# One decode step on one core: the last row of wo with the weight stationary and the output on 128 partitions

## The chip, the cores and the metric

The kernel runs on one core of a Trainium2 chip. Its time is the device time of one execution in microseconds (us); the time before is a median of 3 runs.

## The reference

One token passes through an attention block and an MLP that work in parallel on the same normalised input, and their outputs are added to it:

```python
x = A_x                                   # 1 x 1 x 1024
xn = _layernorm(x)
return x + _A_ref(xn, k_cache, v_cache, wq, wo) + _B_ref(xn, w1, b1, w2, b2)
# A: q = xn @ wq, 32 heads of 128; scores against the last 4096 positions of 4 kv heads,
#    softmax, o = p @ v (4096 numbers), then o @ wo
# B: y = layernorm(xn); h = gelu(y @ w1 + b1) with the tanh form, 3584 numbers; h @ w2 + b2
```

Everything is bf16. The weights, keys and values are about 40 MB and each is read once, for a single token.

## The kernel before

**Loads.** The large transfers go through the queue of SP in a fixed order: k_sb (4 pieces), wq (2), w1 (2), v_sb (3), w2 (2), wo (6). They land in tiles of one pool with four slots, so each later transfer waits until an earlier tile is used up: the last six pieces (L228) need the slots of w1 and v_sb. The 32 rows of wo that a partition holds come as one piece of 16 rows and then as pieces of 8, 4, 2, 1 and 1 rows. The small inputs go through the queue of ACT: x as 128 partitions of 8 numbers (x_sb, L75), x and b2 again as rows of 512 (xb2, L78 and L79), and b1 as one row of 3584 on one partition (b1_row, L81).

**Stages.** The layer norms (L123 to L170) use matmuls with ones for sums over partitions. The keys are transposed on DVE in blocks of 32x32 (L185) and moved to their places by 64 copies, 26 of them on ACT (L199) and 38 on DVE (L201). The queries are 64 matmuls into accq (L237), two PSUM banks, which DVE (L240) and ACT (L241) then copy to q_sb, one bank each; L261 transposes them on TensorE. The hidden layer is 64 matmuls into acch (L257), begun by 8 matmuls of one row that put b1 there (L249). Scores, softmax and p @ v follow (L275 to L319, o_all). In the time of o_all, ACT computes Gelu on acch (L312) and DVE transposes the result to columns, hT (L314). The head outputs become columns too, o8 (L331).

**The output sums.** All 28 rows of w2 and 32 rows of wo, called chunks, are multiplied in order with a column of hT or o8 as the stationary operand, one column wide, and the weight row as the moving operand. The first 52 chunks, the bulk, go to accf (L338): two matmuls of 512 columns each, on partitions 0 and 32 of one PSUM bank. accf was begun by two matmuls that put x + b2 there (L177). The last 8 chunks, rows 24 to 31 of wo, go to acct (L353), four matmuls of 256 columns on partitions 0, 32, 64 and 96. While these run, the bulk is copied to bulk on the same four partitions, by DVE (L348) and ACT (L350) in turn. One add (L356) of acct and bulk on 97 partitions gives res, and four of its rows are stored (L357).

```python
for t in range(4):
    half, w = divmod(t, 2)
    src = accf[32 * half:32 * half + 1, 256 * w:256 * w + 256]
    if w == 0:
        nc.vector.tensor_copy(out=bulk[32 * t:32 * t + 1, :], in_=src)
    else:
        nc.scalar.copy(out=bulk[32 * t:32 * t + 1, :], in_=src)
```

The order on each engine is the program's, apart from instructions that a scheduler places earlier because nothing holds them.

Of the kernel before, what the change touches and what calls it, by code (L numbers as in the profile page):

```python
# [8 lines left out]
FP32 = mybir.dt.float32  # L9
BF16 = mybir.dt.bfloat16  # L10
ACT = mybir.ActivationFunctionType
ALU = mybir.AluOpType
# [4 lines left out]
def kernel(  # L17
# [14 lines left out]
    nc = tc.nc  # L32
    P = 128
# [7 lines left out]
    Fd = B_w1.shape[1]  # L41
    W = min(4096, max(256, Sk // 4))
    C = D // P
# [3 lines left out]
    CW2 = Fd // P  # L47
    CWO = NQ // P
    TAIL = 8
    NH = Fd // 8  # L50
    eps = 1e-5
    scale = float(Dh) ** -0.5
    assert Dh == P and D == 1024 and Hkv == 4 and Hq == 32 and NQ == 4096 and Fd == 3584 and W == 4096

    consts = ctx.enter_context(tc.tile_pool(name="consts", bufs=1))
    small = ctx.enter_context(tc.tile_pool(name="small", bufs=2))
# [10 lines left out]
    x_flat = A_x.rearrange("a b d -> (a b d)")  # L67
# [8 lines left out]
    xb2 = consts.tile([34, 512], BF16)  # L76
    nc.gpsimd.memset(xb2[:], 0.0)
    nc.scalar.dma_start(out=xb2[0:33:32, :], in_=x_flat.rearrange("(t n) -> t n", t=2))  # L78
    nc.scalar.dma_start(out=xb2[1:34:32, :], in_=B_b2.rearrange("(t n) -> t n", t=2))  # L79
    b1_row = consts.tile([1, Fd], BF16)  # L80
    nc.scalar.dma_start(out=b1_row[:], in_=B_b1.rearrange("(a n) -> a n", a=1))  # L81
# [90 lines left out]
    accf = ps_acc.tile([P, 512], FP32, tag="accf")  # L172
    accq = ps_acc.tile([P, 2, 512], FP32, tag="accq", name="accq")
    nc.vector.memset(accq[:], 0.0)
    for half in range(2):
        pr = 32 * half
        nc.tensor.matmul(accf[pr:pr + 1, :], lhsT=ones_bf[pr:pr + 2, 0:1], rhs=xb2[pr:pr + 2, :],  # L177
                         start=True, stop=False, tile_position=(pr, pr))
# [10 lines left out]
    for g in range(Hkv):  # L189
        T4 = scr[:, g, :].rearrange("p (c a j) -> p c a j", a=4, j=32)  # L190
        k = 0
# [6 lines left out]
    for (dst, src) in act_moves:  # L198
        nc.scalar.copy(out=dst, in_=src)  # L199
    for (dst, src) in dve_moves:  # L200
        nc.vector.tensor_copy(out=dst, in_=src)  # L201
# [21 lines left out]
    for i, cuts in enumerate([[0, 16], [0, 8, 12, 14, 15, 16]]):  # L223
        nr = CWO // 2
        t = ring_tile(f"wo{i}")
        tv = t[:].rearrange("p (r n) -> p r n", r=nr)
        for a, b in zip(cuts[:-1], cuts[1:]):
            nc.sync.dma_start(out=tv[:, a:b, :], in_=wo_v[:, nr * i + a:nr * i + b, :])  # L228
        chunk_src += [("o", nr * i + r, tv[:, r, :]) for r in range(nr)]

# [16 lines left out]
    for j in range(8):  # L247
        t, b = divmod(j, 2)
        nc.tensor.matmul(acch[32 * t:32 * t + 1, b, :NH], lhsT=ones_bf[0:1, 0:1], rhs=b1_row[:, j * NH:(j + 1) * NH],  # L249
                         start=True, stop=False, tile_position=(0, 32 * t))  # L250
    for i, w3 in enumerate(w1_tiles):
        for r in range(4):
            c = 4 * i + r
            for b in range(2):
                for t in range(4):
                    j = 2 * t + b
                    nc.tensor.matmul(acch[32 * t:32 * t + 1, b, :NH], lhsT=yT[:, c:c + 1], rhs=w3[:, r, j * NH:(j + 1) * NH],  # L257
                                     start=False, stop=(c == C - 1), tile_position=(0, 32 * t))
# [49 lines left out]
    h_sb = consts.tile([P, 2 * NH], BF16)  # L308
    zcol = small.tile([P, 1], FP32, tag="zcol")
    nc.vector.tensor_scalar_mul(out=zcol[:], in0=l_loc[:], scalar1=0.0)  # L310
    for b in range(2):
        nc.scalar.activation(out=h_sb[:, b * NH:(b + 1) * NH], in_=acch[:, b, :NH], func=ACT.Gelu_apprx_tanh, bias=zcol[:])  # L312
    hT = consts.tile([P, CW2, 32], BF16)
    nc.vector.transpose(out=hT[:], in_=h_sb[:].rearrange("p (d c) -> p c d", c=CW2))  # L314
# [19 lines left out]
    vec = {"h": lambda c: hT[:, c, 0:1], "o": lambda c: o8[:, c:c + 1]}  # L334
    n_bulk = len(chunk_src) - TAIL
    for idx, (kind, c, wap) in enumerate(chunk_src[:n_bulk]):
        for half in range(2):
            nc.tensor.matmul(accf[32 * half:32 * half + 1, :], lhsT=vec[kind](c), rhs=wap[:, half * 512:(half + 1) * 512],  # L338
                             start=False, stop=(idx == n_bulk - 1), tile_position=(0, 32 * half))
    acct = ps_f.tile([P, 256], FP32, tag="pf", name="acct")  # L340
    nc.vector.memset(acct[:], 0.0)
    bulk = consts.tile([97, 256], FP32)
    nc.gpsimd.memset(bulk[:], 0.0)
    for t in range(4):
        half, w = divmod(t, 2)
        src = accf[32 * half:32 * half + 1, 256 * w:256 * w + 256]
        if w == 0:
            nc.vector.tensor_copy(out=bulk[32 * t:32 * t + 1, :], in_=src)  # L348
        else:
            nc.scalar.copy(out=bulk[32 * t:32 * t + 1, :], in_=src)  # L350
    for idx, (kind, c, wap) in enumerate(chunk_src[n_bulk:]):
        for t in range(4):
            nc.tensor.matmul(acct[32 * t:32 * t + 1, :], lhsT=vec[kind](c), rhs=wap[:, t * 256:(t + 1) * 256],  # L353
                             start=(idx == 0), stop=(idx == TAIL - 1), tile_position=(0, 32 * t))
    res = consts.tile([97, 256], BF16)
    nc.vector.tensor_tensor(out=res[:], in0=acct[0:97, :], in1=bulk[:], op=ALU.add)  # L356
    nc.sync.dma_start(out=out.rearrange("a b (t n) -> (a b t) n", t=4), in_=res[0:97:32, :])  # L357
# [30 lines left out]
```

## Time and profile before

| | |
|---|---|
| median of 3 runs | 102.42 us (102.39 to 102.57) |
| span of the profiled execution, first to last instruction | 100.7 us |
| median less span | 1.7 us |
| moved | 39.92 MB, mean 396 GB/s over the span |
| busy: PE, PE loads, DVE, ACT, POOL | 49.1, 19.2, 49.4, 34.2, 4.5 us |
| mean granted TensorE clock | 0.766 |
| last row of wo used by PE | from 97.36 us |
| last add on DVE | 97.76 us, 0.42 us |
| store issued on SP | 98.21 us, 0.63 us |

The profiled execution has no time of its own on record beside its span; the 1.7 us is what the median of the three runs lies above that span. In the profile PE is the matmul part of TensorE and PEld its loading of stationary operands; a letter q behind an engine means its queue, which waits and issues transfers. L338 is line 338 of the kernel before. "x64" counts instructions. The DMA rows give packets, MB and the share of the 16 DMA engines; q1 is the queue of SP, q10 that of ACT, and q8 carries the fetches of instructions.

### The profile page before, as it was taken

The numbers are of one execution on the slowest core, as the hardware profiler recorded it, in microseconds if no ns is written. First come the engines' busy times: TensorE is split into PE (matmuls) and PEld (weight loads), VectorE is DVE, ScalarE is ACT, GpSimd is POOL, SyncE is SP. The second block draws the span as 40 slices with busy tenths as digits, with TensorE's granted clock in tenths as the row PEclk, the third lists the DMA queues.
The fourth block names the chain that finished last, engine by engine and source line by source line (L and its number), as shares of the span: only waits on it lengthen the run. The fifth ranks groups of instructions, "written<-read, shape, count | busy, mean of one in ns | idle before, by whom it ended". The sixth has DMA issues, their size and how long they took to land.

```text
span 100.7 us, 962 instructions
## 1 busy us (share of the span) xinstructions
PE 49.1 (49%) x361; PEld 19.2 (19%) x361; DVE 49.4 (49%) x91; ACT 34.2 (34%) x37; POOL 4.5 (4%) x18
## 2 busy tenths in 40 slices
PE   0027200008500930482882935999389930299830
PEld 0012200003100300121531222334133410023310
DVE  4335499999999999997126115510630000000130
ACT  0500002999999999962001045400000000000110
POOL 7105300000000000000000000000000000000000
PEclk9999999999985579555555555569976997559995
DMA  3899999999999998999999998999999998999910
GB/s 52 346 434 436 482 443 482 443 430 417 417 417 391 456 444 376 459 444 382 391 423 430 436 511 387 467 428 433 433 410 413 456 456 384 423 420 408 369 33 1
DMA packets 3031, 39.92 MB, mean 396 GB/s; under 512 B 458, under 2 KB 466, under 8 KB 851
## 3 DMA queue, kind: packets, MB, share of 16 engines
q1 hardware_dynamic: 2872, 39.85, 93.3%
q8 instruction: 3, 0.05, 0.2%
q10 hardware_dynamic: 154, 0.01, 0.1%
q14 instruction: 2, 0.01, 0.0%
HBM read 39.86 MB, written 0.00 MB: 396 GB/s over the span
## 4 chain that ended last, share of the span: by engine, by line
DVE 37%; DMA 24%; PE 19%; issue 9%; POOL 3%; ACT 2%; SPq 2%; POOLq 1%; DVEq 0%; ACTq 0%
DMA wo<-in_A_wo_dram 24%; DVE kt_scr L185 17%; DVE kT L201 16%; PE o_all L319 10%; PE sp L275 4%; PE acch L257 3%; SPq L228 2%; ACT e L297 1%; DVE eTb L299 1%; DVE m_loc L283 1%; PE qT_ps L261 1%; DVE q_sb L240 1%; POOLq L383 1%; ACT sc L280 1%; POOL spread L113 1%
## 5 line engine op out<-in xcount | busy, mean ns | idle before, releaser
L199 ACT COPY kT<-kt_scr 32x1024 bf16<-32x1024 bf16 x26 | 27.1, 1042 | 12.9 <-DVE kt_scr L185 12.6
L185 DVE STREAM_TRANSPOSE kt_scr<-k_sb 128x4096 bf16<-128x4096 bf16 x4 | 17.4, 4412 | 0.0
L201 DVE COPY kT<-kt_scr 32x1024 bf16<-32x1024 bf16 x38 | 15.9, 419 | 0.5
L237 PE MATMUL accq<-wq,xnT 128*1 128x512 bf16 x64 | 7.1, 622 | 17.9 <-DMA wq<-in_A_wq_dram 17.9
L350 ACT COPY bulk<-accf 1x256 f32<-1x256 f32 x2 | 0.7, 361 | 31.7 <-DVE bulk L348 31.7
L348 DVE COPY bulk<-accf 1x256 f32<-1x256 f32 x2 | 0.8, 416 | 21.3 <-PE accf L338 20.8
L319 PE MATMUL o_all<-v_sb,eTb 128*32 128x512 bf16 x32 | 9.9, 485 | 1.0 <-DVE zcol L310 1.0
L338 PE MATMUL accf<-wo,o 128*1 128x512 bf16 x48 | 7.1, 465 | 6.1 <-DMA wo<-in_A_wo_dram 6.1
L257 PE MATMUL acch<-w,yT 128*1 128x448 bf16 x64 | 6.3, 574 | 5.6 <-DMA w<-in_B_w_dram 5.6
L338 PE MATMUL accf<-w,hT 128*1 128x512 bf16 x56 | 7.9, 452 | 0.0
L237 PEld LDWEIGHTS <-xnT 128*1 128x1 bf16 x64 | 2.1, 115 | 22.1 <-issue 22.1
L319 PEld LDWEIGHTS <-eTb 128*32 128x32 bf16 x32 | 3.7, 119 | 6.8 <-issue 3.8
L338 PEld LDWEIGHTS <-o 128*1 128x1 bf16 x48 | 2.4, 98 | 10.8 <-issue 8.9
L275 PE MATMUL sp<-kT,qm 128*32 128x512 bf16 x32 | 3.8, 629 | 0.3 <-DVE qm L266 0.3
L257 PEld LDWEIGHTS <-yT 128*1 128x1 bf16 x64 | 2.0, 116 | 9.4 <-issue 9.4
L131 PE MATMUL ln_tot<-st,ones_f 128*128 128x1 f32 x2 | 0.6, 362 | 6.4 <-DVE st L129 6.4
L338 PEld LDWEIGHTS <-hT 128*1 128x1 bf16 x56 | 2.7, 96 | 4.7 <-issue 2.3
L322 DVE TENSOR_TENSOR o_m<-o_all,grs 32x512 f32<-32x512 f32 x1 | 0.7, 679 | 5.6 <-PE o_all L319 5.6
L297 ACT ACTIVATE e<-sc,nmx 128x1024 bf16<-128x1024 f32 x1 | 1.1, 1147 | 5.7 <-DVE nmx L294 5.7
L314 DVE STREAM_TRANSPOSE hT<-h_sb 128x896 bf16<-128x896 bf16 x1 | 1.7, 1711 | 2.4 <-ACT h_sb L312 2.4
L261 PE MATMUL qT_ps<-ident,q_sb 128*128 128x128 bf16 x8 | 1.2, 308 | 2.3 <-DVE q_sb L240 2.3
L275 PEld LDWEIGHTS <-qm 128*32 128x32 bf16 x32 | 2.1, 133 | 1.4 <-issue 0.9
(84 smaller groups left out, 34.4 us busy)
## 6 DMA issues: line engine op xcount, KB each, us to landing
w<-in_B_w_dram SPq DMA_DIRECT2D x4, 3584.0 KB, 26.1
wq<-in_A_wq_dram SPq DMA_DIRECT2D x2, 4096.0 KB, 21.6
k_sb<-in_A_k_cache_dram SPq DMA_DIRECT2D x4, 1024.0 KB, 7.1
wo<-in_A_wo_dram SPq DMA_DIRECT2D x1, 4096.0 KB, 29.4
v_sb<-in_A_v_cache_dram SPq DMA_DIRECT2D x1, 2048.0 KB
v_sb<-in_A_v_cache_dram SPq DMA_DIRECT2D x2, 1024.0 KB, 23.4
wo<-in_A_wo_dram SPq DMA_DIRECT2D x1, 2048.0 KB
wo<-in_A_wo_dram SPq DMA_DIRECT2D x1, 1024.0 KB, 23.1
```

The lines of the kernel that those rows point to most:

```text
L185: nc.vector.transpose(out=scr[:, g, :], in_=k2[:, g, :])
L199: nc.scalar.copy(out=dst, in_=src)
L201: nc.vector.tensor_copy(out=dst, in_=src)
L228: nc.sync.dma_start(out=tv[:, a:b, :], in_=wo_v[:, nr * i + a:nr * i + b, :])
L237: nc.tensor.matmul(accq[32 * t:32 * t + 1, b, :], lhsT=xnT[:, c:c + 1], rhs=w3[:, r, j * 512:(j + 1) * 512], start=(c == 0), stop=(c == C ...
L257: nc.tensor.matmul(acch[32 * t:32 * t + 1, b, :NH], lhsT=yT[:, c:c + 1], rhs=w3[:, r, j * NH:(j + 1) * NH], start=False, stop=(c == C - 1) ...
L261: nc.tensor.transpose(qT_ps[:, b * 4 + hh, :], q_sb[:, b, hh * Dh:(hh + 1) * Dh], ident[:])
L275: nc.tensor.matmul(sp[32 * R:32 * R + 32, :], lhsT=qm[:, g, :], rhs=kT[:, g, c0:c0 + 512], start=(g == 0), stop=(g == Hkv - 1), tile_posit ...
L297: nc.scalar.activation(out=e128[:], in_=sc[:], func=ACT.Exp, bias=nmx[:], scale=scale, accum_out=l_loc[:])
L314: nc.vector.transpose(out=hT[:], in_=h_sb[:].rearrange("p (d c) -> p c d", c=CW2))
L319: nc.tensor.matmul(o_all[:].rearrange("h g d -> h (g d)"), lhsT=eTb[:, 32 * c:32 * c + 32], rhs=v4[:, :, c, :], start=(c == 0), stop=(c == ...
L338: nc.tensor.matmul(accf[32 * half:32 * half + 1, :], lhsT=vec[kind](c), rhs=wap[:, half * 512:(half + 1) * 512], start=False, stop=(idx == ...
```

## The change

The last row of wo (row 31) is used the other way round: eight blocks of 128 of its columns are loaded as the stationary operand, and the column of o8 is the moving operand, so that the outputs lie on 128 partitions, 8 on each (accr). The row arrives in two halves. The other sums are brought to the same layout: the bulk, now in two PSUM banks (accf takes over the tile of accq), is copied by DVE (first half) and ACT (second half), transposed on DVE (bulkT), added to x + b2 (bx) and put into accr by an identity matmul ahead of row 29; acct, rows 24 to 30, is transposed on DVE (acctT) and added at the end. The store writes 4 numbers for each partition and half.

b1, b2 and x are loaded as 128-partition tiles (b1_sb, b2h, xh) instead of rows; b2 in two parts, of 72 and 56 partitions, from ACT's queue behind its fourth and eighth copy of keys. The ten matmuls that put the biases and x into PSUM are gone. The hidden layer is transposed first, on DVE from PSUM (hx); b1 is added and Gelu is computed on 128x28 numbers as h / (1 + exp(-2c(h + 0.044715 h^3))), with Exp on ACT and the rest on DVE.

```diff
+    GELU_C = 0.7978845608028654
...
     x_sb = consts.tile([P, C], BF16)
     nc.scalar.dma_start(out=x_sb[:], in_=x_flat.rearrange("(p c) -> p c", p=P))
-    xb2 = consts.tile([34, 512], BF16)
-    nc.gpsimd.memset(xb2[:], 0.0)
-    nc.scalar.dma_start(out=xb2[0:33:32, :], in_=x_flat.rearrange("(t n) -> t n", t=2))
-    nc.scalar.dma_start(out=xb2[1:34:32, :], in_=B_b2.rearrange("(t n) -> t n", t=2))
-    b1_row = consts.tile([1, Fd], BF16)
-    nc.scalar.dma_start(out=b1_row[:], in_=B_b1.rearrange("(a n) -> a n", a=1))
+    xh = consts.tile([P, 2, 4], BF16)
+    nc.scalar.dma_start(out=xh[:], in_=x_flat.rearrange("(r p j) -> p r j", r=2, p=P))
+    b1_sb = consts.tile([P, CW2], BF16)
+    nc.scalar.dma_start(out=b1_sb[:], in_=B_b1.rearrange("(p c) -> p c", p=P))
+    b2h = consts.tile([P, 2, 4], BF16)
...
-    accf = ps_acc.tile([P, 512], FP32, tag="accf")
     accq = ps_acc.tile([P, 2, 512], FP32, tag="accq", name="accq")
     nc.vector.memset(accq[:], 0.0)
-    for half in range(2):
-        pr = 32 * half
-        nc.tensor.matmul(accf[pr:pr + 1, :], lhsT=ones_bf[pr:pr + 2, 0:1], rhs=xb2[pr:pr + 2, :],
-                         start=True, stop=False, tile_position=(pr, pr))
...
-    for (dst, src) in act_moves:
+    b2_v = B_b2.rearrange("(r p j) -> p r j", r=2, p=P)
+    for k, (dst, src) in enumerate(act_moves):
         nc.scalar.copy(out=dst, in_=src)
+        if k in (3, 7):
+            p0, p1 = (0, 72) if k == 3 else (72, P)
+            nc.scalar.dma_start(out=b2h[p0:p1, :, :], in_=b2_v[p0:p1, :, :])
     for (dst, src) in dve_moves:
         nc.vector.tensor_copy(out=dst, in_=src)
...
-    for i, cuts in enumerate([[0, 16], [0, 8, 12, 14, 15, 16]]):
+    for i, cuts in enumerate([[0, 16], [0, 8, 12, 14, 15]]):
         nr = CWO // 2
         t = ring_tile(f"wo{i}")
         tv = t[:].rearrange("p (r n) -> p r n", r=nr)
         for a, b in zip(cuts[:-1], cuts[1:]):
             nc.sync.dma_start(out=tv[:, a:b, :], in_=wo_v[:, nr * i + a:nr * i + b, :])
         chunk_src += [("o", nr * i + r, tv[:, r, :]) for r in range(nr)]
+        if i == 1:
+            for hc in range(2):
+                nc.sync.dma_start(out=tv[:, 15, hc * 512:(hc + 1) * 512], in_=wo_v[:, 31, hc * 512:(hc + 1) * 512])
...
     acch = ps_acc.tile([P, 2, 512], FP32, tag="acch", name="acch")
     nc.vector.memset(acch[:], 0.0)
-    for j in range(8):
-        t, b = divmod(j, 2)
-        nc.tensor.matmul(acch[32 * t:32 * t + 1, b, :NH], lhsT=ones_bf[0:1, 0:1], rhs=b1_row[:, j * NH:(j + 1) * NH],
-                         start=True, stop=False, tile_position=(0, 32 * t))
     for i, w3 in enumerate(w1_tiles):
         for r in range(4):
             c = 4 * i + r
@@ -255,7 +253,7 @@
                 for t in range(4):
                     j = 2 * t + b
                     nc.tensor.matmul(acch[32 * t:32 * t + 1, b, :NH], lhsT=yT[:, c:c + 1], rhs=w3[:, r, j * NH:(j + 1) * NH],
-                                     start=False, stop=(c == C - 1), tile_position=(0, 32 * t))
+                                     start=(c == 0), stop=(c == C - 1), tile_position=(0, 32 * t))
...
-    h_sb = consts.tile([P, 2 * NH], BF16)
-    zcol = small.tile([P, 1], FP32, tag="zcol")
-    nc.vector.tensor_scalar_mul(out=zcol[:], in0=l_loc[:], scalar1=0.0)
-    for b in range(2):
-        nc.scalar.activation(out=h_sb[:, b * NH:(b + 1) * NH], in_=acch[:, b, :NH], func=ACT.Gelu_apprx_tanh, bias=zcol[:])
-    hT = consts.tile([P, CW2, 32], BF16)
-    nc.vector.transpose(out=hT[:], in_=h_sb[:].rearrange("p (d c) -> p c d", c=CW2))
+    hx = consts.tile([P, CW2, 32], FP32)
+    nc.vector.transpose(out=hx[:].rearrange("p c (b i) -> p c b i", b=2),
+                        in_=acch[:, :, :NH].rearrange("p b (i c) -> p c b i", c=CW2))
+    hp = small.tile([P, CW2], FP32, tag="hp")
+    nc.vector.tensor_tensor(out=hp[:], in0=hx[:, :, 0], in1=b1_sb[:], op=ALU.add)
+    hc = small.tile([P, CW2], FP32, tag="hc")
+    nc.vector.tensor_scalar(out=hc[:], in0=hp[:], scalar1=-10.0, scalar2=None, op0=ALU.max)
+    h2 = small.tile([P, CW2], FP32, tag="h2")
+    nc.vector.tensor_tensor(out=h2[:], in0=hc[:], in1=hc[:], op=ALU.mult)
+    nc.vector.tensor_scalar(out=h2[:], in0=h2[:], scalar1=0.044715, scalar2=1.0, op0=ALU.mult, op1=ALU.add)
+    nc.vector.tensor_tensor(out=h2[:], in0=h2[:], in1=hc[:], op=ALU.mult)
+    he = small.tile([P, CW2], FP32, tag="he")
+    nc.scalar.activation(out=he[:], in_=h2[:], func=ACT.Exp, scale=-2.0 * GELU_C)
+    nc.vector.tensor_scalar(out=he[:], in0=he[:], scalar1=1.0, scalar2=None, op0=ALU.add)
+    hr = small.tile([P, CW2], FP32, tag="hr")
+    nc.vector.reciprocal(out=hr[:], in_=he[:])
+    hT = consts.tile([P, CW2], BF16)
+    nc.vector.tensor_tensor(out=hT[:], in0=hp[:], in1=hr[:], op=ALU.mult)
+    xb = consts.tile([P, 2, 4], FP32)
+    nc.vector.tensor_tensor(out=xb[:], in0=xh[:], in1=b2h[:], op=ALU.add)
...
-    vec = {"h": lambda c: hT[:, c, 0:1], "o": lambda c: o8[:, c:c + 1]}
+    vec = {"h": lambda c: hT[:, c:c + 1], "o": lambda c: o8[:, c:c + 1]}
     n_bulk = len(chunk_src) - TAIL
+    accf = ps_acc.tile([P, 2, 512], FP32, tag="accq", name="accf")
     for idx, (kind, c, wap) in enumerate(chunk_src[:n_bulk]):
+        w4 = wap.rearrange("p (r h u) -> p h r u", r=2, h=2)
         for half in range(2):
-            nc.tensor.matmul(accf[32 * half:32 * half + 1, :], lhsT=vec[kind](c), rhs=wap[:, half * 512:(half + 1) * 512],
-                             start=False, stop=(idx == n_bulk - 1), tile_position=(0, 32 * half))
+            nc.tensor.matmul(accf[32 * half:32 * half + 1, half, :].rearrange("a (r u) -> a r u", r=2), lhsT=vec[kind](c),
+                             rhs=w4[:, half], start=(idx == 0), stop=(idx == n_bulk - 1), tile_position=(0, 32 * half))
     acct = ps_f.tile([P, 256], FP32, tag="pf", name="acct")
     nc.vector.memset(acct[:], 0.0)
-    bulk = consts.tile([97, 256], FP32)
+    bulk = consts.tile([P, 2, P], FP32)
     nc.gpsimd.memset(bulk[:], 0.0)
-    for t in range(4):
-        half, w = divmod(t, 2)
-        src = accf[32 * half:32 * half + 1, 256 * w:256 * w + 256]
-        if w == 0:
-            nc.vector.tensor_copy(out=bulk[32 * t:32 * t + 1, :], in_=src)
-        else:
-            nc.scalar.copy(out=bulk[32 * t:32 * t + 1, :], in_=src)
-    for idx, (kind, c, wap) in enumerate(chunk_src[n_bulk:]):
+    for w in range(2):
+        for half in range(2):
+            t = 2 * half + w
+            src = accf[32 * half:32 * half + 1, half, :].rearrange("a (r w u) -> a w r u", r=2, w=2)[:, w]
+            if half == 0:
+                nc.vector.tensor_copy(out=bulk[32 * t:32 * t + 1, :, :], in_=src)
+            else:
+                nc.scalar.copy(out=bulk[32 * t:32 * t + 1, :, :], in_=src)
+    bulkT = consts.tile([P, 2, 4, 32], FP32)
+    nc.vector.transpose(out=bulkT[:], in_=bulk[:].rearrange("p r (i j) -> p r j i", j=4))
+    bx = consts.tile([P, 2, 4], FP32)
+    nc.vector.tensor_tensor(out=bx[:], in0=bulkT[:, :, :, 0], in1=xb[:], op=ALU.add)
+    accr = ps_f.tile([P, 2, 4], FP32, tag="pf", name="accr")
+    for idx, (kind, c, wap) in enumerate(chunk_src[n_bulk:-1]):
+        if idx == TAIL - 3:
+            nc.tensor.matmul(accr[:].rearrange("p r j -> p (r j)"), lhsT=ident_f[:], rhs=bx[:].rearrange("p r j -> p (r j)"),
+                             start=True, stop=False, skip_group_check=True)
+        w4 = wap.rearrange("p (r t u) -> p t r u", r=2, t=4)
         for t in range(4):
-            nc.tensor.matmul(acct[32 * t:32 * t + 1, :], lhsT=vec[kind](c), rhs=wap[:, t * 256:(t + 1) * 256],
-                             start=(idx == 0), stop=(idx == TAIL - 1), tile_position=(0, 32 * t))
-    res = consts.tile([97, 256], BF16)
-    nc.vector.tensor_tensor(out=res[:], in0=acct[0:97, :], in1=bulk[:], op=ALU.add)
-    nc.sync.dma_start(out=out.rearrange("a b (t n) -> (a b t) n", t=4), in_=res[0:97:32, :])
+            nc.tensor.matmul(acct[32 * t:32 * t + 1, :].rearrange("a (r u) -> a r u", r=2), lhsT=vec[kind](c), rhs=w4[:, t],
+                             start=(idx == 0), stop=(idx == TAIL - 2), tile_position=(0, 32 * t))
+    acctT = consts.tile([P, 2, 4, 32], FP32)
+    nc.vector.transpose(out=acctT[:], in_=acct[:].rearrange("p (r i j) -> p r j i", r=2, j=4))
+    kind, c, wap = chunk_src[-1]
+    w5 = wap.rearrange("p (r q j) -> p r j q", r=2, j=4)
+    for r in range(2):
+        for j in range(4):
+            nc.tensor.matmul(accr[:, r, j:j + 1], lhsT=w5[:, r, j, :], rhs=vec[kind](c),
+                             start=False, stop=True, skip_group_check=True)
+    res = consts.tile([P, 2, 4], BF16)
+    nc.vector.tensor_tensor(out=res[:], in0=accr[:], in1=acctT[:, :, :, 0], op=ALU.add)
+    nc.sync.dma_start(out=out.rearrange("a b (r p j) -> (a b p) r j", r=2, p=P), in_=res[:])
```

## The prediction

> **What bounds the kernel now.** I read the page first, then the chain of waits, then the timeline of the last 7 us, then the DMA answers by window. The page's span and its DMA row:
>
> ```profile
> span 100.7 us, 962 instructions
> DMA  3899999999999998999999998999999998999910
> ```
>
> The transfers are 90% busy in nearly every slice from 2.5 us to 95 us, so nothing that is merely computed earlier pays. The chain of waits says the same of the end: it is one 24 us wait for the last pieces of wo, and behind it only three steps.
>
> ```profile
> 73.20 24.12 DMA wo<-in_A_wo_dram
> 97.32 0.04 issue
> 97.36 0.31 PE acct L353 x4
> ...
> 97.76 0.42 DVE res L356
> ```
>
> The timeline of the same stretch shows what runs beside that wait:
>
> ```profile
> 94.70 0.41 DVE L348 COPY bulk<-accf 1x256 f32<-1x256 f32 x1 [20.79 <-PE accf L338]
> 95.20 0.36 ACT L350 COPY bulk<-accf 1x256 f32<-1x256 f32 x1 [31.17 <-DVE bulk L348]
> 95.59 0.42 DVE L348 COPY bulk<-accf 1x256 f32<-1x256 f32 x1 [0.48 <-ACT bulk L350]
> 96.05 0.36 ACT L350 COPY bulk<-accf 1x256 f32<-1x256 f32 x1 [0.48 <-DVE bulk L348]
> 96.10 0.39 PE L353 MATMUL acct<-wo,o 128*1 128x256 bf16 x8 [0.61 <-DMA wo<-in_A_wo_dram]
> 96.73 0.28 PE L353 MATMUL acct<-wo,o 128*1 128x256 bf16 x4 [0.24 <-DMA wo<-in_A_wo_dram]
> 98.21 0.63 SPq L357 DMA_DIRECT2D out_dram<-res  x1
> ```
>
> Two things are to be seen. The four copies of the bulk sums run strictly one after another, each naming the other engine's copy as its releaser: 94.70 to 96.41, 1.71 us. Today that is hidden, since only the last add (97.76) needs them. And wo's rows arrive in steps: rows 28 and 29 at 96.10, row 30 at 96.73, row 31 at 97.36.
>
> Two DMA answers, of 2 to 4 us and of 66 to 68 us (queue, packets, MB, share of 16 engines):
>
> ```profile
> q10 hardware_dynamic: 56, 0.00, 1.6%
> ...
> q8 instruction: 1, 0.02, 2.9%
> ```
>
> In the first, 56 packets, nearly all 16-byte pieces of x, take 1.6% of 16 x 2 us, or 9.1 ns each. In the second, one fetch of instructions takes 2.9% of 32 us, 0.93 us on one engine. From 96 to 97 us only 25 packets move, about what two engines carry: the stream ends on two late engines, about 0.8 us after the rest. I infer that they are the ones that served the fetches near 46 and 67 us.
>
> **The change, part by part.** I work in the profiled execution's times (span 100.7 us) and add the difference to the median of 102.42, taking the 1.7 us outside the span as unchanged.
>
> *Small loads.* Removed: four 1 KB pieces and one of 7 KB. Added: 256 pieces of 8 B (x), 128 of 56 B (b1), 256 of 8 B (b2). Spread over 16 engines that is 16 + 8 + 16 pieces and about 4 completion writes, 44 x 9.1 ns = 0.40 us per engine. If the parts of b2 (72 and 56 partitions, neither divisible by 16) reach 12 and 14 engines, it is 0.24 to 0.44 us. What is removed is 9.2 KB on one or two engines, at most 0.35 us (some 430 GB/s in the full slices, so 27 per engine), and nothing shows these to be the late ones. As the stream has no gap, the late engines pass this on in full: +0.40 us at row 31 and at all arrivals before it, bounds -0.1 and +0.44. Row 31 as 1 KB pieces adds a completion write and eight more packet starts per engine, 0.05 us.
>
> *Moved to places with cover.* The two b2 loads sit in ACT's queue behind its fourth and eighth copy; at about 0.5 us of issue each (ACT's four today take 0.41 to 0.56) they delay the later kT copies by 1 us. ACT ended those at 44.47, DVE at 46.47, so 2 us of cover; beyond it, each us delays the queries. The ten bias matmuls (0.9 and 1.2 us, L249 and L177) leave an idle PE: nothing. The two Gelu calls, the table load of 1.28 us and the 1.71 us transpose become one transpose of 128x896 and ten small DVE steps of 0.16 us with one Exp: 1.7 + 1.6 + 0.3 = 3.6 us from 61.7, over at 65.5. They queue ahead of o_m, which waits for o_all until 71.4; cover 6 us. The adds that wait for b1 and b2 stand there too; those loads, issued by 26 us, have 35 us to land. The extra DMA on SP (0.43 us at 73 us) goes ahead of 24 us of queued data: nothing.
>
> *The bulk sums.* New behind the four copies: a transpose of 128x256 fp32, the add bx, and an identity matmul that the PE must run before row 29. No fp32 transpose is in the trace; bounds are 0.27 us (the clearing of the same shape, L341) and 0.49 us (256 x 1.91 ns, the strided L314 per column); I take 0.30, near the 1.08 ns per column of L185. bx is 0.17 (L138, same width). The identity matmul is fp32 with 128 columns of weights: L131 occupies PE for 0.59, and its first load can go ahead; I take 0.45. The PE queue behind it holds rows 29, 30 and 31, and the add waits for all.
>
> Whether the copies still run in turn decides. The halves now lie in two PSUM banks, one per engine. One place of the trace already has that: accq, two banks, read by DVE and by ACT.
>
> ```profile
> 46.50 0.69 DVE L240 CAST q_sb<-accq 128x512 bf16<-128x512 f32 x1
> 47.22 0.58 ACT L241 CAST q_sb<-accq 128x512 bf16<-128x512 f32 x1 [2.75 <-DVE q_sb L240]
> ```
>
> ACT had been idle since 44.47 and still waited for DVE, though it read the other bank. So I take the copies as serial. With everything 0.40 later: copies 95.10 to 96.81; transpose to 97.15; bx to 97.36; identity matmul to 97.84; rows 29 and 30 in 0.39 (the x8 row above) to 98.23. The transpose of acct, 0.30, runs beside row 31's eight matmuls.
>
> *Row 31.* Before: 4 matmuls, 0.31. Now eight loads of 128 columns with one moving column. Nearest rows: L329, four pairs in 0.25 us at full clock; L261, four pairs with 128 columns in 0.62 at half clock, of which 0.31 is the last one's own length, so 0.10 a pair. Eight take 0.40 (bounds 0.33 and 0.95, strided weights being unseen). They end at 98.63.
>
> The TensorE page (TensorE: Matmul & The Clock Gate, Part 3, "What overlaps and what doesn't") says a load overlaps running matmuls only when its row group differs, and these all use every row. Fully exposed at L261's 0.13 + 0.31 a pair, the sum would be some 3 us longer for eight; L261's four pairs in 0.62 speak against it.
>
> *The last add and the store.* 128x8 instead of 97x256: 0.17 instead of 0.42. It starts at 98.70 and ends at 98.87, against 98.18 today: +0.69. The store's issue falls from 0.63 to about 0.44 (L90, 128 partitions: 0.33 to 0.44). Its 4 pieces of 512 B (25 to 29 ns) become 256 of 8 B, 16 per engine: 0.15 us at the 9 ns of small reads, 0.45 at 28 ns, so +0.1 to +0.4. Net -0.1, bounds -0.2 and +0.2.
>
> The DMA page (DMA: Bandwidth & Descriptors, Specifications) says that below 512 B an engine does read-modify-write; no row here shows a small write, and its price stays open.
>
> Sum: +0.69 - 0.09 = +0.60, 103.0 us.
>
> **Rivals.** *Two banks free the copies* (102.55 us): they take 0.85 us and end at 95.95; bx is there at 96.5 and the identity matmul is over at 97.15, about when row 30 comes. Then only row 31 counts: second half in at 97.36 + 0.45 = 97.81, four matmuls 0.35, add to 98.4, +0.22, store -0.09. The kT moves, which ACT and DVE write side by side, speak for it; L241 against. If b2's pieces and b1's spare the late engines, this case falls to 102.2.
>
> *The late engines change* (101.8 us, faster): the PE runs 20 fewer instructions before the tail, so its fetches come later. If one no longer falls into the stream, or a late engine is relieved otherwise, row 31 arrives up to 0.8 us sooner. That decides once bx is ready before row 30; against it, both fetches lie 28 us and more before the stream's end, and 20 PE instructions are 1 to 3 us.
>
> *The store or the fetch costs more* (103.9 us): 256 writes of 8 B into the same 2 KB hold each other up by 1 us, or both fetches meet on one engine (+0.93).
>
> **How the numbers follow.** Serial copies 0.42, free copies 0.33, late engines 0.12, dear store 0.13. This kernel's times separate about 0.2%, 0.2 us. Free copies give 0.07 faster, 0.21 same, 0.05 slower; serial ones 0.02 same, the rest slower. Faster 0.19, same 0.23, slower 0.58. The serial case alone spans 102.75 to 103.4; the range reaches down through the free copies to 102.0 and up to 103.5.
>
> **What would show it.** In the new profile: q10 with about 700 packets; row 31 at 97.7 to 97.9; L348 and L350 in turn (serial) or side by side; PE idle ahead of row 29, released by bx; Gelu's table load gone; the add at 0.17 us; a store issue near 0.44. Row 31 arriving before 97.4, or a PE that never waits for bx, would make the forecast wrong.

## The result, and the profile after

After: 119.52 us (median of 3, 119.11 to 119.73) against 102.41 us before on the same chip; ratio 1.167, 95% interval 1.163 to 1.172. Medians and ratios leave out runs more than 1.5% above the fastest of the same kernel: one of 121.14 us here and one of 106.49 us in experiment 1. Slower, as forecast, but by 17.1 us instead of 0.6, and far outside the range. The profiled execution took 119.73 us with a span of 117.9.

The page after, its span, DMA share and bandwidth in 40 slices of 2.95 us:

```profile
span 117.9 us, 964 instructions
DMA  2999999999900599405798999999999989899700
GB/s 56 412 342 429 476 422 445 445 445 411 389 0 0 156 457 447 185 6 146 321 428 370 414 428 433 461 438 457 438 418 408 500 389 478 361 411 404 301 13 0
```

The stream of weights, which before had no gap, now runs dry twice, near 33 to 39 us and 48 to 55 us. Against some 0.9 in a full slice the DMA row misses 4.2 slices between the 12th and the 20th, 12 us. DVE's timeline after tells why (start, duration, engine, line, operation; in brackets the idle time before it and its releaser):

```profile
8.65 0.16 DVE L143 TENSOR_SCALAR ve<-ln_tot 128x1 f32<-128x1 f32 x1 [0.68 <-PE ln_tot L141]
33.86 0.17 DVE L325 TENSOR_TENSOR xb<-xh,b2h 128x8 f32<-128x8 bf16 x1 [25.05 <-DMA b2h<-in_B_b_dram]
33.95 0.36 DVE L181 TENSOR_REDUCE sel<-ident_f 128x32 f32<-128x128 f32 x1
34.22 0.22 DVE L146 TENSOR_SCALAR xn_f<-xc,rstd 128x8 f32<-128x8 f32 x1
...
37.08 4.44 DVE L180 STREAM_TRANSPOSE kt_scr<-k_sb 128x4096 bf16<-128x4096 bf16 x1
```

Line 325, the add of x and b2 that stands behind Gelu in the program, runs between lines 143 and 146 of the first layer norm: its operands come from loads alone, so the scheduler had put it there. DVE stood 25.05 us before it, and the transposes of the keys, at 12.61 us before, begin at 37.08. The same had been there to see in the profile before, on the timeline of DVE: line 186, 40 lines further down, sits in the same gap of the layer norm.

```profile
8.50 0.16 DVE L143 TENSOR_SCALAR ve<-ln_tot 128x1 f32<-128x1 f32 x1 [0.68 <-PE ln_tot L141]
8.58 0.36 DVE L186 TENSOR_REDUCE sel<-ident_f 128x32 f32<-128x128 f32 x1
9.33 0.25 DVE L146 TENSOR_SCALAR xn_f<-xc,rstd 128x8 f32<-128x8 f32 x1 [0.40 <-POOL rstd L145]
```

Nor did the loads of b2 stay behind ACT's fourth and eighth copy. ACT's timeline after has them at 2.30 us, behind b1's:

```profile
1.72 0.48 ACTq L80 DMA_DIRECT2D b_sb<-in_B_b_dram  x1
2.30 1.38 ACTq L198 DMA_DIRECT2D b2h<-in_B_b_dram  x2
```

Issued by 3.7 us, they still landed only at 33.8. The DMA answer for 16 to 30 us after (queue, packets, MB, share of 16 engines) shows how the pieces moved:

```profile
q1 hardware_dynamic: 201, 6.06, 100.2%
q10 hardware_dynamic: 164, 0.00, 0.7%
```

One large packet lasts 100.2% of 16 x 14 us divided by 201, 1.12 us, and in that time hardly one small piece moves. q10's 842 packets are 768 pieces and 74 completion writes, 3 x 16 for x_sb, xh and b1 and 26 for b2: its parts went to 12 and 14 engines, 144/12 = 12 pieces from the one and 112/14 = 8 from the other. An engine with both has 22 small packets of b2 to move, at one beside each packet of wq. The trace's packets show wq used up near 33 us, and then the rest went through at once.

SP's waits after name what ran dry with it: line 205, the loads of w1, and line 219, those of w2, need slots that DVE and PE were late to free.

```profile
SPq L205 <- DVE kt_scr L180: 15.2, 1, 15.2
SPq L205 <- PE accq L239: 14.9, 1, 14.9
SPq L219 <- DVE kT L200: 14.0, 1, 14.0
```

The last stretch of the timeline after answers to the one of before:

```profile
110.22 0.84 DVE L362 COPY bulk<-accf 1x256 f32<-1x256 f32 x2 [13.21 <-PE accf L351]
110.31 0.73 ACT L364 COPY bulk<-accf 1x256 f32<-1x256 f32 x2 [26.13 <-PE accf L351]
...
111.17 0.63 DVE L366 STREAM_TRANSPOSE bulkT<-bulk 128x256 f32<-128x256 f32 x1
111.83 0.17 DVE L368 TENSOR_TENSOR bx<-bulkT,xb 128x8 f32<-128x8 f32 x1
...
112.05 0.39 PE L372 MATMUL accr<-bx,ident_f 128*128 128x8 f32 x2 [0.69 <-DVE bx L368]
...
112.92 0.64 PE L384 MATMUL accr<-o,wo 128*128 128x1 bf16 x8
112.95 0.45 DVE L379 STREAM_TRANSPOSE acctT<-acct 128x256 f32<-128x256 f32 x1 [0.96 <-PE acct L376]
113.59 0.17 DVE L387 TENSOR_TENSOR res<-accr,acctT 128x8 bf16<-128x8 f32 x1 [0.19 <-PE accr L384]
113.78 0.40 SPq L388 DMA_DIRECT2D out_dram<-res  x1
```

The copies run side by side, and the PE waits 0.69 us for bx. The store is issued by 114.18, its last packet ends at 114.95, and the span at 117.94, 2.99 us later; before, these were 98.84, 99.54 and 100.70, so 1.16.

### The profile page after: what moved, and what is told of

It is laid out like the page before. It is cut to its first block, busy times and chain, and to the rows that moved or that the text cites. A ratio compares the mean times of both kernels' runs of the same rounds, so it can differ in the third digit from the quotient of the medians.

```text
span 117.9 us, 964 instructions
## 1 busy us (share of the span) xinstructions
PE 41.0 (35%) x357; PEld 17.9 (15%) x357; DVE 50.6 (43%) x102; ACT 31.8 (27%) x35; POOL 4.0 (3%) x17
## 4 chain that ended last, share of the span: by engine, by line
DVE 34%; issue 29%; PE 17%; DMA 12%; POOL 3%; ACT 2%; POOLq 1%; DVEq 0%; ACTq 0%
DVE kt_scr L180 15%; DVE kT L200 13%; DMA wo<-in_A_wo_dram 12%; PE o_all L330 8%; PE sp L273 3%; PE acch L255 2%; PE accf L351 2%; ACT e L295 1%; DVE eTb L297 1%; DVE m_loc L281 1%; PE qT_ps L259 1%; DVE bulk L362 1%; DVE q_sb L242 1%; DVE bulkT L366 1%; PE accr L384 1%
## 5 line engine op out<-in xcount | busy, mean ns | idle before, releaser
L159 PE MATMUL ln_tot<-st,ones_f 128*128 128x2 f32 x2 | 0.6, 362 | 26.4 <-DVE st L157 26.4
L330 PE MATMUL o_all<-v_sb,eTb 128*32 128x512 bf16 x32 | 9.1, 454 | 1.0 <-DVE rs L301 1.0
L351 PE MATMUL accf<-w,hT 128*1 128x512 bf16 x56 | 6.2, 379 | 0.0
L351 PE MATMUL accf<-wo,o 128*1 128x512 bf16 x48 | 5.5, 378 | 1.8 <-DMA wo<-in_A_wo_dram 1.8
L239 PE MATMUL accq<-wq,xnT 128*1 128x512 bf16 x64 | 5.0, 478 | 0.0
L159 PEld LDWEIGHTS ln_tot<-st,ones_f 128*128 128x128 f32 x2 | 0.5, 309 | 26.5 <-DVE st L157 26.5
L259 PEld LDWEIGHTS <-q_sb 128*128 128x128 bf16 x8 | 0.7, 130 | 19.8 <-DVE q_sb L242 19.5
L273 PE MATMUL sp<-kT,qm 128*32 128x512 bf16 x32 | 3.2, 556 | 0.4 <-DVE qm L264 0.4
```

Of the source, the lines that this page charges most:

```text
L239: nc.tensor.matmul(accq[32 * t:32 * t + 1, b, :], lhsT=xnT[:, c:c + 1], rhs=w3[:, r, j * 512:(j + 1) * 512], start=(c == 0), stop=(c == C ...
L259: nc.tensor.transpose(qT_ps[:, b * 4 + hh, :], q_sb[:, b, hh * Dh:(hh + 1) * Dh], ident[:])
L273: nc.tensor.matmul(sp[32 * R:32 * R + 32, :], lhsT=qm[:, g, :], rhs=kT[:, g, c0:c0 + 512], start=(g == 0), stop=(g == Hkv - 1), tile_posit ...
L330: nc.tensor.matmul(o_all[:].rearrange("h g d -> h (g d)"), lhsT=eTb[:, 32 * c:32 * c + 32], rhs=v4[:, :, c, :], start=(c == 0), stop=(c == ...
L351: nc.tensor.matmul(accf[32 * half:32 * half + 1, half, :].rearrange("a (r u) -> a r u", r=2), lhsT=vec[kind](c), rhs=w4[:, half], start=(i ...
```

## The experiments

Each experiment is a kernel of its own; times are medians, beside runs of the kernel before on the same chip (102.33 to 102.38). "The gap" is the time from the last packet of the store to the end of the span.

**Experiment 1: the add of x and b2 only behind the transposed bulk.**

```diff
-    nc.vector.tensor_tensor(out=xb[:], in0=xh[:], in1=b2h[:], op=ALU.add)
...
-    nc.vector.tensor_tensor(out=bx[:], in0=bulkT[:, :, :, 0], in1=xb[:], op=ALU.add)
+    nc.vector.tensor_tensor(out=bx0[:], in0=bulkT[:, :, :, 0], in1=xh[:], op=ALU.add)
+    nc.vector.tensor_tensor(out=bx[:], in0=bx0[:], in1=b2h[:], op=ALU.add)
```

> The changed kernel, but x and b2 are added to the bulk sums one after the other behind bulkT, so no DVE instruction asks for b2 before the tail. Wait theory (DVE stands 25.05 us in front of the add xb until b2 has landed, and everything from the first layer norm on is late by that): the first transpose of the keys starts near 12.8 us again and the time falls from 119.6 to 104.7 us = 102.4 + 0.4 for the small packets + 0.2 in the tail + 1.7 for a slower completion of the store (2.9 us from the store's last packet to the end of the span, against 1.25 before); 103.0 if the slow completion has another cause. Rival (the 8-byte loads themselves slow the stream and the start): still above 110 us, the stream well under 400 GB/s in the first 30 us.

Measured 105.54 us (104.81 to 106.18), ratio 1.031 [1.025, 1.037]; the profiled execution took 106.49 us. On its timeline the transposes are back in their place:

```profile
12.72 4.44 DVE L180 STREAM_TRANSPOSE kt_scr<-k_sb 128x4096 bf16<-128x4096 bf16 x1
```

So the place of one add of 0.17 us carried 119.52 - 105.54 = 14.0 of the 17.1 us. The remaining 3.1 us were more than the 2.3 that the wait theory had.

**Experiments 2 and 5: the early add kept, b2's load with fewer pieces on an engine.** In 2 b2 is one transfer of 256 pieces; in 5 one of 128 pieces of 16 bytes.

```diff
-            p0, p1 = (0, 72) if k == 3 else (72, P)
-            nc.scalar.dma_start(out=b2h[p0:p1, :, :], in_=b2_v[p0:p1, :, :])
+            nc.scalar.dma_start(out=b2h[:], in_=b2_v)    # experiment 2
+            nc.scalar.dma_start(out=b2h[:].rearrange("p r j -> p (r j)"), in_=B_b2.rearrange("(p q) -> p q", p=P))    # experiment 5
```

> The changed kernel with b2 loaded in one part on 128 partitions, so 16 pieces and 1 completion per engine instead of 12 + 8 and 2 on the busiest; the early add xb stays. Wait theory (one small packet passes for each 32 KB packet of wq, 1.2 us): 5 packets fewer, the add comes 6 us earlier (near 28 us instead of 33.9) and the time falls by about as much, to 113.6 us (113 to 115). Rival (the number of small pieces sets the loss, 512 pieces of 8 bytes in both): 119.6 us, no change.

> The changed kernel with its early add xb, but b2 in one part of 128 pieces of 16 bytes, 8 and 1 completion per engine (its numbers come to other places, so the output is not the sum wanted). In the runs so far the add was released at 33.9 us (22 packets of b2 per engine) and 32.6 us (17): both times when the 16 packets of 32 KB of wq per engine were used up and the stream ran dry. Wait theory with that cap: one packet of b2 passes per packet of wq, 1.2 us, so 9 packets from 13.7 us are through at 24.5 us, the add starts there, 9.4 us earlier than in the changed kernel; w1's first load is then issued before the stream runs dry, and only its second, which waits for the last key transpose (54.5 us there, 45.1 us here), finds it dry, for 4 to 5 us: 111 us (109 to 113). Rival (a fixed loss by the early add, not by how long b2 takes): 119.3 us.

Experiment 2: 119.25 us, no gain worth the name, where 113.6 was expected. That is near the rival's number, but the rival's reason, the number of small pieces, does not hold: experiment 1 loads as many and takes 14 us less. Experiment 5: 110.90 us, as expected. DVE's timelines, of 2 and then of 5:

```profile
32.59 0.17 DVE L324 TENSOR_TENSOR xb<-xh,b2h 128x8 f32<-128x8 bf16 x1 [23.84 <-DMA b2h<-in_B_b_dram]
```

```profile
23.86 0.17 DVE L324 TENSOR_TENSOR xb<-xh,b2h 128x8 f32<-128x8 bf16 x1 [15.10 <-DMA b2h<-in_B_b_dram]
```

b1 lands near 13.8 us in the kernel after. From there, at 1.12 us a turn, 16 pieces and a completion write need 19.0 us (to 32.8; measured 32.6), 8 pieces and one 10.1 us (to 23.9; measured 23.9). Both fit one small packet per large one, and the DMA answer for 16 to 30 us of experiment 2 counts just that:

```profile
q1 hardware_dynamic: 202, 6.09, 100.8%
q10 hardware_dynamic: 202, 0.00, 0.8%
```

The expectation for 2 failed since it took the full 22 turns for the kernel after, which had been cut short when wq ran out.

**Experiment 3: the loads, biases and Gelu of before, only the tail of the change.** x and b2 are again put into accf by two matmuls; the copies, both transposes, the identity matmul, row 31 as the stationary operand and the 8-byte store are those of the change.

```diff
     nc.scalar.dma_start(out=xb2[0:33:32, :]..., in_=x_flat...)      # rows, in the new order of columns
     nc.tensor.matmul(accf[pr:pr + 1, half, :], lhsT=ones_bf[pr:pr + 2, 0:1], rhs=xb2[pr:pr + 2, :], ...)
-    nc.vector.tensor_tensor(out=bx[:], in0=bulkT[:, :, :, 0], in1=xb[:], op=ALU.add)
+    nc.vector.tensor_copy(out=bx[:], in_=bulkT[:, :, :, 0])
```

> The kernel before with its own loads, biases and Gelu, and only the tail of the change: bulk sums in two banks and transposed, identity matmul, row 31 with the weight stationary, store of 256 pieces of 8 bytes. x + b2 enter the bulk sums by the two matmuls of before, placed ahead of the bulk. Wait theory: the tail has no part in the 17 us; 102.4 + 0.2 (tail) + 1.7 (store) = 104.3 us. Rival (tail free, the small loads cost): 102.4 us. Rival (tail at the root of the loss): above 110 us.

Measured 104.11 us, ratio 1.019 [1.014, 1.023], as expected. Its timeline at the end:

```profile
95.25 0.84 DVE L353 COPY bulk<-accf 1x256 f32<-1x256 f32 x2 [22.80 <-PE accf L342]
...
97.83 0.42 PE L375 MATMUL accr<-o,wo 128*128 128x1 bf16 x8
97.95 0.45 DVE L370 STREAM_TRANSPOSE acctT<-acct 128x256 f32<-128x256 f32 x1 [0.92 <-PE acct L367]
98.50 0.17 DVE L378 TENSOR_TENSOR res<-accr,acctT 128x8 bf16<-128x8 f32 x1
98.70 0.40 SPq L379 DMA_DIRECT2D out_dram<-res  x1
```

The last piece of wo lands at 96.95, as before (96.99), but row 31 is used only from 97.83: from the end of the bulk the chain of copies, transpose, bx, identity matmul, rows 29 and 30 and the second transpose is 3.4 us long and now sets the end. The last add ends 0.5 us later than before (98.67 against 98.18). The bulk itself ended later too: its copies begin at 95.25 against 94.70. From 87.5 to 92 us PE was busy for 4.49 of 4.50 us at a granted clock of 0.50, where before it had 0.60. Counted from 94.70, the 3.4 us would end at 98.1, level with before; so much of the 0.5 us may be the clock of this execution and not the tail, and no run here holds the clock equal. The gap is 2.70.

**Experiment 4: experiment 1 with the store of before.**

```diff
-    nc.sync.dma_start(out=out.rearrange("a b (r p j) -> (a b p) r j", r=2, p=P), in_=res[:])
+    nc.sync.dma_start(out=out.rearrange("a b (t n) -> (a b t) n", t=4), in_=res[0:97:32, :])
```

> Like the late add, but the store is that of before, 4 pieces of 512 bytes from partitions 0, 32, 64 and 96 of a cleared tile into which the last add writes its 8 columns; so most of the output is left out. If the 8-byte pieces cost a slow completion: 1.7 us less than the late add (near 103.0 us), with the end of the span 1.25 us behind the store's last packet. If the slow completion comes of something else: the same as the late add within 0.3 us.

Measured 104.46 us, 1.08 below experiment 1, where 1.7 was expected; the two profiled executions (106.49 and 104.45 us) differ by 2.0. The gap falls from 3.55 to 1.32, of which 0.2 is given back in a longer issue on SP.

**Experiment 7: the kernel before with only its store cut into 8-byte pieces.** 256 pieces from 4 partitions.

```diff
-    nc.sync.dma_start(out=out.rearrange("a b (t n) -> (a b t) n", t=4), in_=res[0:97:32, :])
+    nc.sync.dma_start(out=out.rearrange("a b (m t u) -> (a b t) m u", t=4, u=4),
+                      in_=res[0:97:32, :].rearrange("t (m u) -> t m u", u=4))
```

> The kernel before with one change: the store goes out as 256 pieces of 8 bytes, 64 from each of the same four partitions (the numbers land in another order). Small-piece theory: it completes slowly as the store of the change does, 2.7 us or more from its last packet to the end of the span instead of 1.2, and 64 packets of 9 ns follow one another on an engine: 102.4 + 1.5 + 0.5 = 104.4 us. Rival (the slow completion comes of 16 engines that each post one, not of the pieces): 102.9 us or less.

Measured 104.95 us, ratio 1.024 [1.020, 1.029], gap 2.81: the small-piece theory, and 0.5 us more than it had. The pieces of the store alone cost 2.6 us here; it has 4 completion writes as before, so their number is not it.

**Experiment 8: the kernel before with the small loads added, unused.** xh, b1_sb and the two parts of b2h, behind its own four loads on ACT's queue.

```diff
+    nc.scalar.dma_start(out=xh[:], in_=x_flat.rearrange("(r p j) -> p r j", r=2, p=P))
+    nc.scalar.dma_start(out=b1_sb[:], in_=B_b1.rearrange("(p c) -> p c", p=P))
+    for p0, p1 in ((0, 72), (72, P)):
+        nc.scalar.dma_start(out=b2h[p0:p1, :, :], in_=b2_v[p0:p1, :, :])
```

> The kernel before plus the four small loads of the change (x, b1 and b2 as 128-partition tiles, 640 pieces), behind its own loads in ACT's queue and used by nothing. Packet theory: 44 to 48 packets of 9 ns per engine, passed on in full by the two late engines: row 31 and the time 0.4 to 0.6 us later, 102.9 us. Rival (all of the 1.75 us between the late add and the new tail alone comes of these loads): 104.1 us. Rival (small packets cost nothing): 102.4 us.

Measured 103.75 us, ratio 1.015 [1.010, 1.021], between the 102.9 of the packet theory and the 104.1 of the first rival: 1.4 us for 640 pieces, over three times what their own 9 ns each make. The DMA answers for 6 to 12 us, first of before, then of experiment 8, show that q1 moved less:

```profile
q1 hardware_dynamic: 347, 2.58, 101.7%
q10 hardware_dynamic: 8, 0.00, 0.2%
```

```profile
q1 hardware_dynamic: 290, 2.11, 94.9%
q10 hardware_dynamic: 704, 0.01, 6.9%
```

The small pieces took 6.9% of the engines, 9.4 ns each as predicted; yet q1 moved 0.47 MB less, and each MB of it took 45.0% of the window instead of 39.4%. By 30 us the stream, counted in whole packets of up to 32 KB, is 0.61 MB behind (11.46 against 12.07), 1.4 us at 0.43 MB per us. Not all of it is the pieces. In this kernel SP's first four transfers are issued only by 8.7 us (2.8 before), and near 7.5 us q1 ran dry, as the bandwidth of the same 6 us in 40 slices of 0.15 us shows (11th slice):

```profile
GB/s 492 382 389 444 437 383 492 383 437 273 7 473 339 166 275 166 328 328 328 219 546 328 546 273 601 273 547 273 329 330 330 330 329 329 383 274 437 273 437 273
```

From 7 to 8 us 371 of q10's packets went through. Experiment 2 has the same 640 pieces and SP done at 2.9 us; by 30 us it is 0.42 MB behind (11.65). By this estimate the pieces cost 1.0 us and SP's late issue 0.4; no run separates them.

**Experiment 6: the loads of before, and 8 neighbouring numbers for each partition.** As experiment 3, but the columns in their natural order, so that the store is 128 pieces of 16 bytes; 16 rows instead of 8 behind the bulk; row 31 in one piece.

```diff
-    TAIL = 8
+    TAIL = 16
...
+    w5 = wap.rearrange("p (q j) -> p j q", j=8)
+    nc.sync.dma_start(out=out.rearrange("a b (p j) -> (a b p) j", p=P), in_=res[:])
```

> The loads, biases and Gelu of before; the tail of the change with 8 neighbouring numbers per partition, so that the store has 128 pieces of 16 bytes; the bulk ends 16 rows before the end instead of 8, so that its copies, transpose and identity matmul are done long before row 29; row 31 in one piece. Chain theory (in the new tail alone the end was set by the bulk sums: 3.4 us from the last bulk matmul to the last add): that chain is now off the path, row 31 is used at 97.4 us, the add ends near 98.0 and is issued 0.2 us faster: 102.0 us if pieces of 16 bytes complete like those of 512, 103.4 us if they complete like those of 8. Rival (the tail is not what made the new tail slow, only the store): 104.1 us less nothing, i.e. like the new tail alone, if 16 bytes cost the same.

Measured 102.08 us (10 runs), ratio 0.998 [0.996, 0.999]: 0.25 us below the kernel before. The longer tail starts the chain earlier, and row 31 waits for its data again.

**Experiment 9: experiment 6 with the rest of the change put back in 16-byte and 56-byte pieces.** x comes from x_sb, b1 and b2 are one load each, Gelu is in columns, both adds stand behind the transposed bulk.

```diff
+    nc.scalar.dma_start(out=b1_sb[:], in_=B_b1.rearrange("(p c) -> p c", p=P))
+    nc.scalar.dma_start(out=b2_sb[:], in_=B_b2.rearrange("(p c) -> p c", p=P))
...
+    nc.vector.tensor_tensor(out=bx0[:], in0=bulkT[:, :, 0], in1=x_sb[:], op=ALU.add)
+    nc.vector.tensor_tensor(out=bx[:], in0=bx0[:], in1=b2_sb[:], op=ALU.add)
```

> The kernel of experiment 6 (8 neighbouring numbers per partition, 16-byte store, 16 rows in the tail) with the rest of the change put back: b1 as 128 pieces of 56 bytes, b2 as 128 pieces of 16 bytes, x taken from x_sb, no bias matmuls, Gelu in columns, and x and b2 added only after the transposed bulk, in two adds. Theory (the small pieces slow the large packets beside them: the 640 pieces of experiment 8 left the stream 0.62 MB, 1.4 us, behind by 30 us, 2.3 ns a piece; three transfers in ACT's queue instead of four; the add no longer waits early): 256 pieces cost 0.4 to 0.6 us, the second add is beside the 16 rows of the tail: 102.5 to 102.7 us, SP's issue of k_sb near 2.0 us, key transposes from about 12.7 us. Rival (only pieces of 8 bytes cost more than their 9 ns; 56 and 16 bytes do not): 102.0 to 102.2, level with experiment 6. Rival (the new Gelu and the adds of b1 cost time on the path to wo): over 103.

Measured 103.56 us, ratio 1.012 [1.009, 1.014], a miss for the theory and the first rival. The second rival's number (over 103) came true, but not its reason: experiment 10 below has the same Gelu and adds and stays at 102.84. The stream was level with before at 30 us (12.07 MB), and the last add ended at 98.32 us against 98.04 in experiment 6, but the gap was 2.34 us with the very store that leaves 1.20 in experiment 6.

**Experiments 10 and 11: experiments 9 and 6 with the 512-byte store.**

```diff
-    nc.sync.dma_start(out=out.rearrange("a b (p j) -> (a b p) j", p=P), in_=res[:])
+    nc.sync.dma_start(out=out.rearrange("a b (t n) -> (a b t) n", t=4), in_=res[0:97:32, :])
```

> Experiment 9 with the store of the kernel before: the last add fills 8 columns of a cleared 128x256 tile, and partitions 0, 32, 64 and 96 of it are stored as 4 pieces of 512 bytes; most of the output is left out. Theory (in experiment 9 the 128 pieces of 16 bytes are completed late: 2.34 us from the last piece to the end of the span, where experiment 6 with the same store shows 1.20 and 512-byte pieces 1.2 to 1.4): 102.4 to 102.6 us, a gap near 1.3. Rival (the end is late in experiment 9 for another reason than the store): 103.5, a gap above 2.

> Experiment 6 with the store of the kernel before, as in experiment 10; most of the output is left out. Theory (in experiment 6 the 16-byte store costs nothing): 102.0 to 102.3 us, level with experiment 6, a gap of 1.2 to 1.4. Rival (experiment 6 pays for its small pieces too, by an earlier end elsewhere): under 101.8.

Experiment 10: 102.84 us, gap 1.23; experiment 11: 102.51 us, ratio 1.001 [1.000, 1.003], gap 1.15; both times are 0.2 us above what was expected. So the late end of experiment 9 was its store's, and the whole rest of the change, well placed, costs 102.84 - 102.51 = 0.33 us. And the gain of experiment 6 is not that of the stationary row: with the old store the new tail is level with before. Most of it goes with the store's issue on SP, first experiment 6, then experiment 11:

```profile
97.17 0.66 PE L368 MATMUL accr<-o,wo 128*128 128x1 bf16 x8 [0.20 <-DMA wo<-in_A_wo_dram]
97.87 0.17 DVE L370 TENSOR_TENSOR res<-accr,acctT 128x8 bf16<-128x8 f32 x1 [0.39 <-PE accr L368]
98.06 0.35 SPq L371 DMA_DIRECT2D out_dram<-res  x1
```

```profile
97.42 0.66 PE L368 MATMUL accr<-o,wo 128*128 128x1 bf16 x8
98.11 0.17 DVE L371 TENSOR_TENSOR res<-accr,acctT 128x8 bf16<-128x8 f32 x1 [0.32 <-PE accr L368]
98.34 0.63 SPq L372 DMA_DIRECT2D out_dram<-res  x1
```

0.35 against 0.63 us, 0.28 of the 0.43 us between the two medians. Row 31 takes 0.66 us in this form where it took 0.31 before, and the add 0.17 instead of 0.42: the two nearly cancel.

## Why the prediction was wrong

The steps add up from the medians: before 102.41, the new tail with its store 104.11 (experiment 3), with the small loads, Gelu and late adds 105.54 (experiment 1), with the early add 119.52: 1.7, 1.4 and 14.0 us. That it would be slower came true largely by luck: most of the chance given to it rested on copies in turn, and they ran side by side.

**The step that failed** is "Moved to places with cover". It took the order of the program for the order of the queues: the adds that wait for b1 and b2 "stand there too", behind 61.7 us of work, and b2's loads behind ACT's fourth and eighth copy, with "35 us to land". The add of x and b2 and the loads of b2 were both placed early, and there the add had 25.05 us of wait in front of the transposes, which nothing covers: 14.0 us of time for a term that the sum put at nothing. Line 186 of the kernel before, seen at 8.58 us, speaks against that step; the prediction asked whether ACT's copies would be late, not where the moved instructions would stand. No rival held it either: all of them change only the last 8 us.

**How long a small load takes** was read from the wrong column. The prediction used the 56 packets from 2 to 4 us only for their 1.6% share. Taken as a rate, 2 to 6 us show this in the profile before:

```profile
q1 hardware_dynamic: 176, 1.31, 80.6%
q10 hardware_dynamic: 146, 0.01, 2.5%
```

About one small packet to one large one; with packets of 1.12 us that makes 22 of them 25 us. The Trainium skill (DMA: Bandwidth & Descriptors, "Queues, rings and completion order") states that each DMA engine takes turns between its queues, a whole packet of typically some 9 to 17 descriptors at a time. The turns are what the trace shows; the size is not: at 9 pieces a turn b2 would be through in three turns, an estimate of 3.4 us by that page, where experiments 2 and 5 fit one piece a turn.

**The small loads** were taken at +0.40 us with 0.44 as the upper bound; 640 pieces measured 1.4 in experiment 8. The price of a piece itself was right (9.4 ns); what the stream loses beside it was missing from the sum, and SP's late issue too. In experiment 10, 256 pieces in two loads, together with Gelu and the second add, cost 0.33.

**The store** was taken at -0.1 us net with 0.2 as the upper bound; it measured +1.1 (experiments 1 and 4) and +2.6 (experiment 7). The issue was right, 0.40 against 0.44; the pieces' own time too, 0.26 us from first to last in the kernel after. What was missing is how long the completion takes after the last piece. The "dear store" rival named the place, at 13% and +1 us; whether the writes hold each other up, as it had it, stays open. The Trainium skill (DMA: Bandwidth & Descriptors, Specifications) says that below 512 bytes an engine does read-modify-write, without a price. Experiment 7 agrees that small pieces cost; experiments 6 and 11, with 16 and 512 bytes and gaps of 1.20 and 1.15, show that they need not; whether the read-modify-write is the reason, no run shows.

**The tail.** "I take the copies as serial" was wrong: side by side in every kernel with the halves in two banks, 0.84 us instead of 1.71. The pair from accq that argued for serial still runs in turn (ACT at 71.69 after DVE's 70.96 + 0.69), so it was no model for these copies; why is open. The fp32 transposes were too cheap: 0.63 and 0.45 against 0.30, above the upper bound of 0.49 for the first. The identity matmul took 0.39 (predicted 0.45), bx 0.17, the last add 0.17, row 31 0.42 where nothing held it (0.40). The errors nearly cancel: experiment 3's last add ends 0.5 us later than before, where the serial case had 0.69 - 0.40 = 0.3 without the loads. That the bulk itself can end later (0.55 us there) was in no term. That a load of weights would be fully exposed, the page's rule weighed in the prediction, is refuted: in experiment 3 the eight loads (97.83 to 98.17) lie within the time of the eight matmuls, and the pairs took 0.42 us, not 3.5.

**The late engines** did not turn up: experiments 3, 6, 9, 10 and 11 end their data between 96.8 and 97.3 us (before 96.99), whatever the PE ran before.

## What to carry to other kernels

An instruction whose operands come from loads alone has no place of its own: find where the scheduler puts its like, and price the wait there by what stands behind it in that queue; if it is not needed early, hang it on a late result. A small load beside a full stream landed here after as many large packets as it had pieces on one engine, so give it few pieces, and count the slowing of the stream with them. Read the end of a kernel down to the store's completion, not to its issue.

## What the runs showed of the hardware

- The completion of a small-piece store varies from kernel to kernel, in one profiled execution of each: gaps of 1.20 (experiment 6) and 2.34 us (experiment 9) for the same 128 pieces of 16 bytes, 2.70 to 4.05 for 8-byte pieces (after and experiments 1, 2, 3, 5, 7), 1.15 to 1.39 for 512 bytes (before and experiments 4, 8, 10, 11). The times of experiments 6 (10 runs) and 9 (6 runs) agree within 0.4 us, so these two gaps are no accident of one execution; the runs of experiment 1 spread over 1.7 us. What decides between 1.20 and 2.34 stays open; the trace shows only that the completion arrives late (2.5 us from issue in experiment 9, 1.4 in experiment 6).
- SP's issue of its first four transfers takes 2.0 to 2.1 us while ACT's queue issues three or four, 5.6 with five (after, 1, 4), 7.9 with eight (experiment 8). SP's timelines of experiment 2 (four) and of the kernel after (five), with the same 256 pieces of b2:

```profile
0.80 2.14 SPq L74 DMA_DIRECT2D k_sb<-in_A_k_cache_dram  x4
```

```profile
0.80 5.63 SPq L74 DMA_DIRECT2D k_sb<-in_A_k_cache_dram  x4
```

  The 5.6 us cost nothing there: both had moved 11.65 MB by 30 us. The 7.9 us of experiment 8 let q1 run dry.
- Eight pairs of a 128-column load and a one-column matmul take 0.42 us with weights read at every fourth number (experiments 1 and 3) and 0.66 us at every eighth (experiments 6, 9, 11). The step of the columns is not the only difference between them, so it is not shown to be the cause.
